# HGRN2 attention and a squared-ReLU layer on one core: chunks taken in pairs, two tokens a partition, loads in rows of 384 bytes, state products beside the score products

## The chip, the core and the metric

One core of a Trainium2 chip runs the whole kernel. The metric is the device time of one launch in microseconds. Before the change: 193.36 us, the median of three runs (192.49 to 193.87). A ratio is the mean time of one kernel's fast runs over that of the kernel before's fast runs of the same rounds on the same chip, so it isn't quite the ratio of the medians that I quote. The chips differ by about half a per cent (the fast runs of the kernel before took 192.8 us on average on one chip, 194.0 on another), so I compare experiments by their ratios.

## The reference

Four sequences of 768 tokens, 8 heads of 48. A gated linear attention, token by token, then a two-layer network over all 3072 tokens:

```python
f = 1.0 / (1.0 + np.exp(-f_logit))
for t in range(S):
    state = f[:, :, t, :, None] * state + np.einsum('bhd,bhe->bhde', k[:, :, t], v[:, :, t])
    y[:, :, t] = np.einsum('bhd,bhde->bhe', q[:, :, t], state)
# y -> x: 3072 tokens x 384
h = np.maximum(x @ w_in, 0.0)        # 384 x 2048
out = h * h @ w_out                  # 2048 x 384
```

## The kernel before

The attention goes in 24 chunks of 128 tokens. For each chunk, TensorE makes a prefix sum of the log gates (p1), ScalarE the exponentials, VectorE multiplies k and q by them; then transposes (p2), scores (p3), outputs (p4) and the state's increment (p5). Several chunks together form a unit of the two-layer network: first layer (h), relu and square on ScalarE and VectorE, second layer (o), store (d).

No engine chooses its order at run time. Each step is declared with a believed duration. A planner simulates the machine with these beliefs and writes one fixed list per engine. On the chip every engine works its list in order, and waits for data at each entry (the longest such wait of TensorE below is 3.7 us, with ready products behind it in the list):

```python
FIRST, RECEIPT = 0.4, 1.2
...
if s.data:                                   # a transfer
    us, size = s.data
    ...
    moved_to = max(moved_to, end + self.FIRST) + us     # one mover, first issued, first landed
fin = moved_to + self.RECEIPT if s.data else end + s.land
```

A load is believed to take 1.07 us and a quarter of a weight matrix 2.4 us, one behind the other. The loads are issued by SyncE, the weights by GpSimd. This is their order; `i` are quarters of the first layer's weights, `o` of the second's, numbers are chunks (f, k, q and v of each):

```python
LOADS = [0, "i0", 1, "i1", 2, "i2", 3, "i3", 4, "o0", "o1", 5, "o2", "o3"] + list(range(6, NCH))

def load(i):
    for n in ("f", "k", "q", "v"):
        def fn(n=n):
            t = io.tile([C, H, D], F32, ...)            # 1024 rows of 192 bytes
            nc.sync.dma_start(t, srcs[n][b].rearrange("h s d -> s h d")[c * C:(c + 1) * C])
        plan.add(f"{n}{i}", "SP", 0.45, fn, take=["io_" + n], rank=0, data=(1.07, 1024))
```

The state products are a step of their own, with 128 rows:

```python
def p5():
    for pr in range(NP):
        nc.tensor.matmul(ds[:, pr, :], a[:, H + 2*pr:H + 2*pr + 2, :]..., vt[:, 2*pr:2*pr + 2, :]...)
```

While TensorE has nothing ready in the first 40 us, the plan puts products of zeros ("fillers") into its list.

## Time and profile before

| profile of the kernel before | |
|---|---|
| span of the profiled run | 189.8 us |
| first first-layer product starts | 17.1 us |
| last product ends | 186.4 us |
| TensorE's products, each until the next one starts | 164.7 us |
| fillers | 13.6 us |
| gaps over 0.25 us between products | 7.0 us |

The last four lines are counted from the start times of TensorE's instructions in the trace; with the 1.0 us before the first one they add up to 186.3. The next lines are the table by stage: stretch, length, busy time (and number of instructions) of PE, PEld, DVE, ACT, POOL, then granted clock, DMA share and GB/s.

```profile
0.00:25.00 25.00, 19.48 (x238) 16.49 (x239) 15.19 (x30) 11.81 (x22) 9.96 (x26) 1.00 1.09 175
25.00:50.00 25.00, 21.95 (x330) 17.93 (x328) 17.72 (x35) 19.43 (x37) 8.14 (x14) 1.00 1.09 179
50.00:100.00 50.00, 49.64 (x568) 33.49 (x565) 43.27 (x86) 40.68 (x93) 18.22 (x33) 1.00 1.03 189
```

TensorE is full from 50 us on, and DMA moves 175 to 179 GB/s in the first two stretches. Two waits of TensorE show how it loses time in its fixed order (engine, line, what it waited for: us in total, times, longest):

```profile
PE hp L444 <- DVE hr L453: 1.9, 1, 1.9
PE pc L286 <- ACT pz L276: 1.8, 3, 1.0
```

The second is the prefix sum waiting for the gates of a later chunk. None of its three waits is over 1.0 us.

### The profile page before, as it was taken

Reading aid. Unit: us, or ns where it says so; the run is one execution under the profiler, and the core shown is the slowest. Engines: PE = TensorE matmul, PEld = TensorE weight load, DVE = VectorE, ACT = ScalarE, POOL = GpSimd, SP = SyncE. Lnnn points to the kernel's source line nnn. Section 1 sums busy time; section 2 is a strip of 40 time slices with the busy share of each in tenths; the row PEclk is TensorE's granted clock in tenths of the full one; section 3 lists DMA queues with packets and bytes.
Section 4 is the critical chain, followed back from the end, with each engine's and each line's share of the span. In section 5 each row is a group of like instructions: output and inputs, shape, how many; then the busy total and the mean of one; then the engine's idle time right before and its main releaser. Section 6 shows DMA issues by size and latency. Waiting matters only on the chain.

```text
span 189.8 us, 4807 instructions
## 1 busy us (share of the span) xinstructions
PE 177.5 (93%) x1845; PEld 120.8 (64%) x1845; DVE 127.6 (67%) x259; ACT 132.8 (70%) x281; POOL 54.8 (29%) x105
## 2 busy tenths in 40 slices
PE   6978689989899999999999999999999999999992
PEld 5867478767676666665656666666565666666551
DVE  5484688668397886999988777777667764343300
ACT  4426479786676469999998986978875787565521
POOL 5451343241224561305324311531324401100000
PEclk9999999999999999999999999999999999999999
DMA  6999899999979999999799999979999762211112
GB/s 122 188 191 206 174 187 153 196 164 191 205 137 221 232 227 201 207 197 159 140 155 194 207 137 241 218 109 215 194 216 177 176 60 64 62 45 41 41 41 83
DMA packets 118646, 30.26 MB, mean 159 GB/s; under 512 B 113408, under 2 KB 117760, under 8 KB 118624
## 3 DMA queue, kind: packets, MB, share of 16 engines
q1 hardware_dynamic: 113760, 23.27, 71.2%
q0 software_dynamic: 4864, 6.69, 16.4%
q8 instruction: 14, 0.23, 0.5%
q14 instruction: 8, 0.07, 0.1%
HBM read 25.17 MB, written 4.72 MB: 157 GB/s over the span
## 4 chain that ended last, share of the span: by engine, by line
PE 75%; ACT 11%; DMA 4%; SPq 3%; DVE 3%; issue 2%
PE op L489 31%; PE hp L444 30%; ACT hr L451 4%; DMA io_f<-in_f_logit_dram 4%; SPq L215 3%; PE at L342 3%; PE yp L365 3%; PE tr L318 2%; ACT hT L458 2%; PE pc L286 2%; PE xp L379 1%; PE ds L405 1%; ACT pz L276 1%; ACT e L275 1%; DVE hr L453 1%
## 5 line engine op out<-in xcount | busy, mean ns | idle before, releaser
L444 PE MATMUL hp<-xT,w_in 128*128 128x384 bf16 (+2 forms) x528 | 78.0, 282 | 2.5 <-DVE hr L453 1.9
L489 PE MATMUL op<-w_out,hT 128*128 128x384 bf16 x384 | 76.2, 326 | 0.3 <-ACT ob L499 0.3
L451 ACT ACTIVATE hr<-hp 128x384 bf16<-128x384 f32 (+1 forms) x100 | 50.5, 509 | 20.0 <-PE hp L444 18.0
L444 PEld LDWEIGHTS <-w_in 128*128 128x128 bf16 x528 | 42.3, 98 | 20.7 <-issue 4.0
L489 PEld LDWEIGHTS <-hT 128*128 128x128 bf16 x384 | 35.1, 98 | 21.8 <-issue 0.4
L460 DVE TENSOR_TENSOR hT<-hr 128x384 bf16<-128x384 bf16 (+1 forms) x75 | 29.7, 400 | 27.7 <-ACT hr L451 26.8
L349 DVE TENSOR_TENSOR am<-at,ut 128x512 bf16<-128x512 f32 x48 | 31.6, 685 | 3.7 <-PE at L342 3.4
L422 POOL TENSOR_TENSOR sz<-tm,en 48x192 bf16<-48x192 f32 x40 | 22.0, 549 | 29.9 <-DVE tm L413 7.2
L458 ACT ACTIVATE hT<-hr 128x384 bf16<-128x384 bf16 (+1 forms) x45 | 24.8, 554 | 1.6 <-DVE hr L453 0.3
L504 POOL DMA_DIRECT2D out_dram<-ob x18 | 10.4, 577 | 47.3 <-ACT ob L499 31.2
L280 POOL CAST vz<-io_v 128x384 bf16<-128x384 f32 x24 | 13.6, 567 | 31.2 <-DMA io_v<-in_v_dram 30.7
L306 DVE TENSOR_TENSOR az<-io_k,ep 128x384 bf16<-128x384 f32 x24 | 14.0, 584 | 8.3 <-ACT ep L296 5.1
L275 ACT ACTIVATE e<-io_f 128x384 f32<-128x384 f32 x24 | 12.5, 520 | 7.7 <-DMA io_f<-in_f_logit_dram 7.7
L499 ACT COPY ob<-op 128x384 f32<-128x384 f32 x18 | 8.6, 478 | 12.8 <-PE op L489 12.7
L296 ACT ACTIVATE ep<-pc 128x384 f32<-128x384 f32 x24 | 11.7, 486 | 5.8 <-PE pc L289 5.4
L310 DVE TENSOR_TENSOR az<-io_q,en 128x384 bf16<-128x384 f32 x24 | 14.7, 614 | 0.0
L276 ACT ACTIVATE pz<-e 128x384 bf16<-128x384 f32 x24 | 12.5, 523 | 0.8
L453 DVE TENSOR_SCALAR hr<-hp 128x384 bf16<-128x384 f32 (+1 forms) x20 | 11.6, 584 | 2.0 <-PE hp L444 1.8
L522 PE MATMUL idle<-zero 128*128 128x128 bf16 x119 | 11.9, 256 | 1.0 <-DVE zero L245 1.0
L302 ACT ACTIVATE en<-pc 128x388 f32<-128x388 f32 (+1 forms) x24 | 11.8, 491 | 0.0
L326 DVE COPY ts<-tr 128x1024 bf16<-128x1024 bf16 x14 | 9.6, 687 | 3.1 <-PE tr L318 2.7
L365 PE MATMUL yp<-vz,am 128*128 128x48 bf16 x192 | 9.5, 184 | 1.3 <-DVE am L349 0.8
(40 smaller groups left out, 149.4 us busy)
## 6 DMA issues: line engine op xcount, KB each, us to landing
io_f<-in_f_logit_dram SPq DMA_DIRECT2D x24, 192.0 KB, 4.5
io_k<-in_k_dram SPq DMA_DIRECT2D x24, 192.0 KB, 4.6
io_q<-in_q_dram SPq DMA_DIRECT2D x24, 192.0 KB, 4.5
io_v<-in_v_dram SPq DMA_DIRECT2D x24, 192.0 KB, 4.5
out_dram<-ob POOLq DMA_DIRECT2D x18, 192.0 KB, 3.5
w_in<-in_moe_w_in_dram POOLq DMA_DIRECT2D x4, 384.0 KB, 7.4
w_out<-in_moe_w_out_dram POOLq DMA_DIRECT2D x4, 384.0 KB, 6.9
out_dram<-ob SPq DMA_DIRECT2D x6, 192.0 KB, 1.9
```

The lines of the kernel that those rows point to most:

```text
L275: nc.scalar.activation(e, st["f", i].rearrange("p h d -> p (h d)"), AFT.Exp, scale=-1.0)
L276: nc.scalar.activation(pz[i % 2][:, :, :D], e.rearrange("p (h d) -> p h d", d=D), AFT.Ln, bias=1.0)
L306: nc.vector.tensor_mul(az[i % 4][:, H:, :D], st["k", i], st["ep", i])
L310: nc.vector.tensor_mul(az[i % 4][:, :H, :D], st["q", i], st["en", i][:, :HD].rearrange("p (h d) -> p h d", d=D))
L349: nc.vector.tensor_mul(t, st["at", i][x], ut4)
L365: nc.tensor.matmul(o_, w, r, start=(n == 0), stop=(n == len(ops) - 1), skip_group_check=True)
L422: nc.gpsimd.tensor_mul(nx[r, :, D * x:D * (x + 1)], st["tm", i][r, :, D * x:D * (x + 1)], st["en", i][r, HD:HD + NP].unsqueeze(2).to_broad ...
L444: nc.tensor.matmul(hp[:, x, :], w_in[:, ks, (f + x) * C:(f + x + 1) * C], xT[:, ks, lo:lo + W], start=(ks == 0), stop=(ks == KS - 1), skip ...
L451: nc.scalar.activation(hr[:, :m, :], st["hp", c0, f][:, :m, :], AFT.Relu)
L458: nc.scalar.activation(st["hT", g][:, f:f + m, lo:lo + W], hr[:, :m, :], AFT.Square)
L460: nc.vector.tensor_mul(st["hT", g][:, f:f + m, lo:lo + W], hr[:, :m, :], hr[:, :m, :])
L489: nc.tensor.matmul(st["o", i], hT[:, fs, tt * C:(tt + 1) * C], w_out[:, fs, :], start=(fs == 0), stop=(fs == FS - 1))
```

## The change

Its intent is to feed the start faster: rows of 384 bytes in place of 192, half as many loads, bigger pieces for ScalarE and VectorE, and state products that share the 64-row mode of the scores. The diff, cut to its core (cuts marked `...`):

```diff
-    LOADS = [0, "i0", 1, "i1", 2, "i2", 3, "i3", 4, "o0", "o1", 5, "o2", "o3"] + list(range(6, NCH))
+    LOADS = [0, 1, "i0", "i1", "i2", "i3", 2, "o0", "o1", "o2", "o3"] + list(range(3, NPR))   # pairs
-    XBAR = 14                                   # transposes by DMA from chunk 14
+    XBAR = 5                                    # from pair 5
-    GC = 3                                      # chunks in a unit
+    GC = 2
...
+                t = io.tile([C, H, 2, D], F32, ...)              # 1024 rows of 384 bytes
+                nc.sync.dma_start(t..., srcs[x][b][:, c*C:(c+2)*C, :].rearrange("h (p r) d -> p h (r d)", r=2))
+            plan.add(f"{x}{n}", "SP", 0.6, fn, take=["io_" + x], rank=0, data=(1.6, 1024))
...
+        def vs():                               # v's half to the other 64 partitions
+            for j in range(2):
+                nc.gpsimd.dma_start(t[b_, j]..., st["vx", n][a_]...)
+        plan.aside.add(f"vs.{n}")
+        plan.add(f"vs.{n}", "POOL", 1.2, vs, after=[f"vs0.{n}"], data=(0.33, 0), rank=-2)
...
+            if state:                           # in p3, first chunk of a pair
+                state()                         # the 16 state products of 64 rows
...
-                (nc.gpsimd if soft else nc.sync).dma_start(out[row:row + C, :], ...)
+                for r in range(2):
+                    (nc.gpsimd if soft else nc.sync).dma_start(out[row + r:row + C:2, :], st["ob", i][P2*r:P2*(r + 1)])
```

The planner itself stays the same but for `aside`: a swap's landing doesn't queue behind other transfers in its beliefs.

## The prediction

> **What bounds the kernel now.** I read the page's busy shares first, then the 40 slices, then the table by stage, then groups by shape, then the timeline.
>
> ```profile
> PE 177.5 (93%) x1845; PEld 120.8 (64%) x1845; DVE 127.6 (67%) x259; ACT 132.8 (70%) x281; POOL 54.8 (29%) x105
> ...
> PE   6978689989899999999999999999999999999992
> ...
> PEclk9999999999999999999999999999999999999999
> DMA  6999899999979999999799999979999762211112
> ...
> q1 hardware_dynamic: 113760, 23.27, 71.2%
> ```
>
> TensorE looks busy everywhere, DMA until about 150 us of 190. Both can't be the bound all the time. So I count useful TensorE work; matmuls in the first 50 us, by shape:
>
> ```profile
> L522 PE MATMUL idle<-zero 128*128 128x128 bf16 x119 | 11.9, 256 | 1.0 <-DVE zero L245 1.0
> L444 PE MATMUL hp<-xT,w_in 128*128 128x128 bf16 x150 | 10.0, 219 | 0.4 <-DVE xT L384 0.3
> L444 PE MATMUL hp<-xT,w_in 128*128 128x256 bf16 x48 | 6.4, 272 | 2.1 <-DVE hr L453 1.9 <-DVE xT L384 0.2
> L318 PE MATMUL tr<-ident,az 128*128 128x128 bf16 x48 | 4.4, 236 | 0.4 <-DVE az L310 0.4
> L489 PE MATMUL op<-w_out,hT 128*128 128x384 bf16 x19 | 4.1, 326 | 0.3 <-ACT ob L499 0.3
> ```
>
> All 119 fillers (products of zeros[...]) lie here, so part of "busy" is waiting. The means include pipeline latency; pace comes from runs of equal products in the chain and the timeline:
>
> ```profile
> 178.60 7.81 PE op L489 x48
> ```
> ```profile
> 17.11 1.47 PE L444 MATMUL hp<-xT,w_in 128*128 128x256 bf16 x12 [0.17 <-DVE xT L384]
> ...
> 21.63 0.94 POOL L280 CAST vz<-io_v 128x384 bf16<-128x384 f32 x1 [6.62 <-DMA io_v<-in_v_dram]
> ```
> ```profile
> 5.49 1.00 SPq L215 DMA_DIRECT2D io_q<-in_q_dram  x1
> 6.53 0.99 SPq L215 DMA_DIRECT2D io_v<-in_v_dram  x1
> 7.57 0.96 SPq L215 DMA_DIRECT2D io_f<-in_f_logit_dram  x1
> ```
>
> A 384-column product costs (7.81-0.326)/47 = 0.16 us; 256 columns (1.47-0.272)/11 = 0.109; 128 columns 0.056 (24 in 1.50 us at 27.54). From starts in the timeline: score block of 8 about 0.42 with the gaps around it, output block of 12 about 0.50, state product 0.045, one-column product 0.055. Useful in the first 50 us: 150 x 0.056 + 48 x 0.109 + 48 x 0.055 (transposes) + 19 x 0.16 + 6 score blocks 2.5 + 6 output blocks 2.8 + the rest 4.0 = 28.5 us. About 21 us are starved. Over the whole run: first layer 62.0 (48, 192 and 288 products of the three widths), second 384 x 0.16 = 61.4, prefix sums 8.2, transposes 6.2, scores 10.1, outputs 11.3, states 3.6, output transposes 3.0: 165.8 us. The last product ends at 178.60 + 7.81 = 186.4, so 20.6 us are not useful, the same 21. After 50 us TensorE is full; the remaining 3.4 us are the last eviction and store. So only the first 50 us can be won, and there inputs set the pace: VectorE, ScalarE and GpSimd are not full, GpSimd waited 6.62 us for a v, and the load queue issues one 192 KB load per 1.03 us, which is the rate at which they drain (191 GB/s).
>
> [...] Near 23.6 us a score block (64-row products) starts about 0.2 us after the last first-layer product's start, not 0.11[...].
>
> **The change, part by part.**
> Loads: 48 of 384 KB in place of 96 of 192 KB, same number of rows per load. [...]1.5 us each: 72 us for all, 99 before. Input and weights up to chunk 5 (4.7 + 3.1 MB) took 42 to 44 us at the 177 GB/s of the first 50 us; with about 230 GB/s some 34 us.
>
> TensorE work: first layer 576 x 0.109 = 63.1 (+1.1, three-chunk units become two-chunk ones); prefix sums 24 x 0.16 + 96 x 0.055 = 9.1 (+0.9); transposes by DMA from chunk 10 and 12 on, not 14 and 18: 80 and 36 remain, -1.8 and -1.0; state products 160 of 64 rows and 96 columns in place of 80. A score block without its gaps has (0.40-0.22)/7 = 0.026 each, with them 0.04; at 0.033 that is 5.3 (+1.7). They share the mode of the scores; the old ones needed no switch, so nothing is removed. Sum +0.9 us, on the path.
>
> VectorE: 12 subtractions x 0.55 = +6.6 us; ScalarE: one exponential less per pair, about -0.2 us x 12. Relu and square go in 96 + 96 pieces of 512, not 120 + 120: 96 x (0.594 + 0.45) = 100, before 117 over both engines. All beside TensorE. GpSimd: v copies 48 x 0.57 = 27 (13.6 before), stores 48 issues less 12 from the load queue, about 21 (10.4), swaps 24 issues x 0.5 = 12: from 55 to about 95 us. Not a bound by share, but it works in order and lies on the start.
>
> The start, step by step. The first f load took 3.1 us from issue to use, 1.03 of it transfer, so f, k, q, v of pair 0 land at 4.3, 5.8, 7.3, 8.8 us. GpSimd: two v copies to 10.0, two swap issues to 11, two more copies to 12.1, four weight issues x 0.83 to 15.4. The weights now start at 12, not 7.5, and run into pair 1's loads: v of pair 1 lands near 18[...]. The program order puts pair 1's copies and swap ahead of the first state update, so that ends at 18 + 1.1 + 1.0 + 1.1 = 21.2. Then the second chunk's output 0.5, copy 0.5, transpose 0.4, copy 0.4, waits 0.2: the first first-layer product starts near 23 us, against 17.1. By then TensorE has done 7 us (three prefix sums, four transposes, three score blocks), so 16 us are idle, against 12.7 before the first product there. After that the old kernel lost another 8; the new one gets data earlier, but in its order the transposes of pair 2 stand between first-layer blocks of pair 0 and need q of pair 2, near 32 us: I put 3 us of stalls. Idle 19, not 20.6: -1.6.
>
> End: the last store is two half transfers, +0.4. Sum: +0.9 - 1.6 + 0.4 = -0.3 us: 193.0.
>
> **The rivals.** (1) Faster input settles it: if GpSimd's order costs less (v of pair 1 lands at 15, state update done at 18), the first product starts near 20 and nothing stalls later; idle 13 to 14, time 187 to 188. For it: DMA full to 150 us, 6.62 us waits for v. Against: TensorE is full after 50 us, so later bandwidth buys nothing. (2) GpSimd becomes the chain: swap and stores ahead of state updates in its order, outputs wait for updates, TensorE stalls in order after 50 us too. For it: GpSimd sat 31.2 us waiting for ob before stores, and its load nearly doubles. Against: 95 of 190 us, and TensorE has other chunks' products. It would add 5 to 10 us: 198 to 203. (3) Four 64-row DMA transposes a pair in place of two of 128 rows: if each keeps the 1.24 us issue, the load queue has 5 + 2.4 + 3.5 = 11 us per pair of 14; loads are up to four pairs ahead, so I expect no more than 1 us.
>
> **Range and chances.** The start decides: first product at 20 to 25 us, later stalls 0 to 6 us, so idle 14 to 24 around 19, and work uncertain by 1. That gives 187.5 to 198.5. Faster by 2% needs under 189.5, idle of about 15.5 in all with the rest as summed: 0.24. Slower needs over 197.2, idle of about 23: 0.22. Within 2%: 0.54.
>
> **What would show it.** Loads: the queue's issue interval near 1.5 us and 384-byte packets at half the count. Work: first-layer groups x576, states x160 at about 0.033. Start: first product of the first layer near 23 us, with GpSimd's state update after pair 1's copies; a time near 20 points to rival 1. Full after 40 us: no stretch with TensorE much under full and no state update that the outputs wait for; if there are any, rival 2. I am wrong if the old kernel's TensorE after 50 us hides stalls that the new order removes, or if 384-byte rows drain no faster by byte than 192.

## The result and the profile after

| | before | after |
|---|---|---|
| time, median of 4 runs (us) | 192.93 (192.03 to 193.87) | 198.8 (197.9 to 199.69) |
| ratio, 95% interval | | 1.030 (1.023 to 1.038) |
| span of the profiled run | 189.8 | 197.1 |
| first first-layer product | 17.1 | 24.3 |
| products | 164.7 | 164.2 |
| fillers | 13.6 | 16.1 |
| gaps over 0.25 us | 7.0 | 11.2 |
| last product ends | 186.4 | 192.7 |

The kernel got slower, by more than my range allowed. The products take no longer; fillers and gaps make the difference. The page after, to be held against the slices in the prediction:

```profile
PE 178.5 (91%) x1951; PEld 134.3 (68%) x1951; DVE 125.8 (64%) x240; ACT 127.9 (65%) x241; POOL 92.4 (47%) x188
...
PE   8866798749999899999999999998999799999991
...
PEclk9999999957999999999999999999999999999999
```

A slice is 4.9 us. The ninth and tenth (39 to 49 us) have a clock of 0.5 and 0.7, and in the ninth TensorE is at 4 tenths. The timeline of TensorE there (start, us, engine, line, operation, operands, count, idle before and its releaser):

```profile
38.18 0.20 PE L422 MATMUL ds<-vx,az 64*128 64x96 bf16 x1
42.09 0.89 PE L333 MATMUL pc<-pz,ut 128*128 128x384 bf16 x2 [3.71 <-ACT pz L295]
42.77 0.39 PE L336 MATMUL pc<-ones,pz 128*128 128x2 bf16 x8
43.03 1.12 PE L583 MATMUL op<-w_out,hT 128*128 128x384 bf16 x3
43.94 2.77 PE L538 MATMUL hp<-xT,w_in 128*128 128x256 bf16 x12
```

TensorE stands still for 3.9 us before a prefix sum, that of pair 3. The twelve first-layer products after it take 2.77 us; in the profile before, twelve of that size took 1.47. That is the half clock: the granted clock is 1.00 from 38.0 to 40.2 us and 0.51 from 40.2 to 47.1, some 7 us at half rate (0.86 on average from 25 to 50 us). It fell 1.8 us into the gap. The length of a gap alone doesn't tell what follows: behind one of 2.4 us in e9 twelve such products took 2.77 us too, while e5, with a stall of 2.7 us, had a mean clock of 0.999. What else sets the clock is not shown. Behind the prefix sum stands ScalarE, and behind it a load:

```profile
40.64 0.84 ACT L293 ACTIVATE e<-io_f 128x768 f32<-128x768 f32 x1 [4.38 <-DMA io_f<-in_f_logit_dram]
```

The load queue tells why that f came so late (SyncE's issues; the second column is how long the queue held the issue):

```profile
8.82 1.44 SPq L224 DMA_DIRECT2D io_v<-in_v_dram  x1
10.31 1.39 SPq L224 DMA_DIRECT2D io_f<-in_f_logit_dram  x1
...
18.05 6.78 SPq L224 DMA_DIRECT2D io_f<-in_f_logit_dram  x1
24.87 5.77 SPq L224 DMA_DIRECT2D io_k<-in_k_dram  x1
30.68 5.59 SPq L224 DMA_DIRECT2D io_q<-in_q_dram  x1
```

Alone, a load of 384 KB starts every 1.47 us on average (from 7.34 to 11.75 us), 267 GB/s. The three issues from 18 us on are held for 6.05 us on average, 65 GB/s, while the eight weight transfers are in flight, from 12.7 to 40.9 us. The DMA view from 18 to 37 us shows how the queues shared (packets, MB, share of 16 engines; q0 has GpSimd's transfers, here almost all weights, q1 the loads):

```profile
q0 software_dynamic: 3158, 2.73, 86.1%
q1 hardware_dynamic: 3154, 1.19, 35.5%
```

The packets went one for one, and the load's are the smaller ones (0.38 KB on average against 0.86): the loads moved 1.19 MB in 19 us, 63 GB/s. In the chain of work that ended last (start, us, what) this is one long piece:

```profile
18.05 22.57 DMA io_f<-in_f_logit_dram
40.62 0.02 issue
40.64 0.85 ACT e L293
41.49 0.02 issue
41.51 0.53 ACT pz L295
42.05 0.04 issue
42.09 0.89 PE pc L333 x2
```

The second layer's weights were issued between 20.8 and 23.8 us, after that f, and the first quarter landed at 32.0, well before it. But the plan has one mover, first issued, first landed: it believed that f was there at 33.3 us and, behind it, put the prefix sum at 36.1 us, ahead of the first second-layer products at 36.6.

### The profile page after: what moved, and what is told of

Its sections match the earlier page's. It is cut to its first block, busy times and chain, and to the rows that moved or that the text cites.

```text
span 197.1 us, 4982 instructions
## 1 busy us (share of the span) xinstructions
PE 178.5 (91%) x1951; PEld 134.3 (68%) x1951; DVE 125.8 (64%) x240; ACT 127.9 (65%) x241; POOL 92.4 (47%) x188
## 3 DMA queue, kind: packets, MB, share of 16 engines
q0 software_dynamic: 6208, 7.87, 19.0%
## 4 chain that ended last, share of the span: by engine, by line
PE 47%; DMA 21%; SPq 10%; DVE 8%; ACT 6%; issue 5%; POOL 2%; DVEq 0%; ACTq 0%; POOLq 0%
PE op L583 22%; PE hp L538 18%; DMA io_f<-in_f_logit_dram 11%; SPq L224 9%; DMA out_dram<-ob 5%; DMA io_q<-in_q_dram 2%; DMA ts<-az 2%; PE yp L484 2%; PE pc L333 2%; DVE am L468 1%; ACT hr L545 1%; SPq L402 1%; DVE az L367 1%; PE at L458 1%; DVE hT L554 1%
## 5 line engine op out<-in xcount | busy, mean ns | idle before, releaser
L538 PE MATMUL hp<-xT,w_in 128*128 128x256 bf16 x576 | 78.5, 276 | 1.5 <-ACT xT L507 1.2
L545 ACT ACTIVATE hr<-hp 128x512 bf16<-128x512 f32 x86 | 50.6, 593 | 33.1 <-PE hp L538 30.1
L538 PEld LDWEIGHTS <-w_in 128*128 128x128 bf16 x576 | 55.0, 99 | 15.9 <-issue 2.4
L554 DVE TENSOR_TENSOR hT<-hr 128x512 bf16<-128x512 bf16 x67 | 30.6, 458 | 32.2 <-ACT hr L545 31.7
L468 DVE TENSOR_TENSOR am<-at,mask 128x512 bf16<-128x512 f32 x48 | 31.4, 679 | 3.1 <-PE at L458 3.1
L306 POOL CAST vx<-io_v 64x384 bf16<-64x384 f32 x24 | 14.8, 618 | 10.3 <-DMA io_v<-in_v_dram 9.3
L552 ACT ACTIVATE hT<-hr 128x512 bf16<-128x512 bf16 x29 | 18.2, 630 | 1.4 <-DVE hr L547 0.6
L325 POOL CAST vz<-io_v 64x384 bf16<-64x384 f32 x24 | 13.1, 547 | 1.2
L617 PE MATMUL idle<-zero 128*128 128x128 bf16 x131 | 12.4, 258 | 1.0 <-DVE zero L255 1.0
L318 POOL DMA_DIRECT2D vz<-vx x24 | 12.8, 538 | 0.0
L295 ACT ACTIVATE pz<-e 128x384 bf16<-128x384 f32 x24 | 11.2, 515 | 0.4
L617 PEld LDWEIGHTS <-zero 128*128 128x128 bf16 x131 | 10.3, 119 | 1.1 <-DVE zero L255 1.0
```

The costliest lines, as they stand in the source:

```text
L306: nc.gpsimd.tensor_copy(st["vx", n][z], vt[z, 1 - j])
L468: nc.vector.tensor_mul(t, st["at", i][x], mask.rearrange("p y s t -> p y (s t)"))
L538: nc.tensor.matmul(hp[:, x, :], w_in[:, ks, (f + x) * C:(f + x + 1) * C], xT[:, ks, lo:lo + W], start=(ks == 0), stop=(ks == KS - 1), skip ...
L545: nc.scalar.activation(hr[:, :m, :], st["hp", c0, f][:, :m, :], AFT.Relu)
L552: nc.scalar.activation(st["hT", g][:, f:f + m, lo:lo + W], hr[:, :m, :], AFT.Square)
L554: nc.vector.tensor_mul(st["hT", g][:, f:f + m, lo:lo + W], hr[:, :m, :], hr[:, :m, :])
```

## The experiments

All 18 runs, e1 to e18 in this order. They changed my theory twice. "Order" means the list of each engine. The results are right unless I say "wrong".

**First theory: the weights' burst, or the work that GpSimd got (rival).** The first run puts the second layer's weights behind pair 3:

```diff
-    LOADS = [0, 1, "i0", "i1", "i2", "i3", 2, "o0", "o1", "o2", "o3"] + list(range(3, NPR))
+    LOADS = [0, 1, "i0", "i1", "i2", "i3", 2, 3, "o0", "o1", "o2", "o3"] + list(range(4, NPR))
```

> The new kernel with the four second-layer weight transfers behind pair 2's v instead of pair 1's. Theory A (the weight burst shuts out pair 3's f load, issued at 18 and landed at 40.6 us, and TensorE then stands 3.7 us and runs two to three us at half clock): f of pair 3 in use before 32 us, no TensorE gap over 1.5 us before 50 us, mean clock back to 1.00, time 192.5 to 194.5. Theory B (what is lost is the start by pairs: first first-layer product at 24.3 us, not 17.1): that start stays and the time moves by less than 1.5, 197.5 to 200. Theory C (GpSimd's order after 50 us): the same, 197.5 to 200.

Measured: 195.97 us, ratio 1.017 (1.009 to 1.026). Pair 3's f landed at 32.1 us, its wait was gone, gaps fell to 9.2 us, but fillers rose to 17.1. About half of the loss.

The second one tells the plan alone that a weight takes longer: `data=(2.4, 0)` becomes `data=(4.0, 0)`.

> The new kernel with only the plan's belief on a weight transfer changed, 4.0 us for 2.4: the same instructions, other order. Theory A in the form that the order trusts in data too early (pair 3's prefix sum at the head of the queue while first-layer work waits behind it): the gap before that prefix sum falls under 1 us, the clock stays up, time 193.5 to 195.5, although f lands as late as before. If the missing data itself starves TensorE: the gap only moves, time 197.5 to 200.

Measured: 201.51 us, 1.047 (1.039 to 1.055). Pair 3's prefix sum, now at 50.1 us, waited for nothing (the one wait of a prefix sum for its gates that is left, 1.7 us, is pair 11's at 149 us). But the gaps after 50 us became ten, 8.1 us in all, against seven and 4.3 us in the changed kernel. The plan now believed that f there at 47.7 us, eight too late (it landed at 39.6), and everything else of the start later too. I read this as "order alone isn't the cure", which was too much: it was another false belief, on all weights at once.

The third delays the DMA transposes: `XBAR = 7`, `XBAR2 = 9` in place of 5 and 6.

> The new kernel with DMA transposes from pair 7 (scores) and 9 (outputs) on, where the kernel before has them, not 5 and 6. Theory D (the load queue stands from 59 to 74 us before pair 5's transposes, DMA runs dry and is late afterwards): the dry stretch goes, time 195 to 197.5. Otherwise TensorE gets 32 + 18 transposes more, 50 x 0.055 = 2.7 us, and the time becomes 199.5 to 202.

Measured: 200.74 us, 1.039 (1.025 to 1.052), and the same stall before pair 3's prefix sum, 2.8 us. The transposes aren't the cause.

The fourth gives the kernel before the new loads alone, 384-byte rows two chunks at a time, the rest as it was (wrong, as the tokens stand in another order):

```diff
+    t = io.tile([C, H, 2, D], F32, ...)   # one load for two chunks, each takes its half
-            plan.add(..., data=(1.07, 1024))
+            plan.add(..., data=(2.14, 1024))
```

> The kernel before with the new loads alone: 48 loads in rows of 384 bytes, chunk r of a pair taking token r of each partition, so the values are those of other tokens and the result is wrong on purpose; all else and the plan's beliefs as before. If faster input is worth something by itself (rival 1 of the prediction): first first-layer product at 15 to 17 us, time 188 to 190.5. If input is not what is missing, or coming in pairs costs what it gains: 191.5 to 194.5. Packets under 512 bytes should halve in either case.

Measured: 193.57 us, 0.998 (0.985 to 1.012). Faster rows alone are worth nothing here: the first product came later (19.7 us in place of 17.1, as a whole pair is loaded first), fillers were 14.3 us.

**Second theory: GpSimd's extra issues.** Each chunk is stored by one transfer of 128 rows (the rows of `out` in the wrong order), order unchanged:

```diff
-                for r in range(2):
-                    (...).dma_start(out[row + r:row + C:2, :], st["ob", i][P2*r:P2*(r + 1)])
+                (...).dma_start(out[row:row + C, :], st["ob", i])
```

> The new kernel with one store a chunk in place of two of 64 rows; the rows of a chunk come out in the wrong order, on purpose; the plan and every other instruction's place are unchanged. Theory C (GpSimd's in-order work after 50 us: each half store costs it 0.55 us of issue, 18 us in all, state updates and store landings behind it make TensorE's 4.3 us of gaps over 0.25 us after 50 us): those gaps fall under 2 us and the ratio to the kernel before to 1.012 to 1.022. If the gaps come from the latency of a pair instead: ratio 1.024 to 1.036 as without the edit (1.030).

Measured: 196.16 us, 1.014 (1.005 to 1.023). It looked like a hit. The trace says otherwise: the gaps (12.2 us) are no smaller than after the change, the last product ends 2.1 us earlier, and the first- and second-layer products took 2.1 us less, because the profiled run never fell to half clock (0.999 on average; its stall at 38 us was 2.7 us, not 3.9). The end is 1.0 us shorter, one store in place of two. So the 3 us were not GpSimd's issue time.

Next, no swap at all; the copies fill all 128 partitions (wrong):

```diff
-                nc.gpsimd.dma_start(t[b_, j]..., st["vx", n][a_]...)     # and the two lines around it
-        plan.add(f"vs.{n}", "POOL", 1.2, vs, after=[f"vs0.{n}"], data=(0.33, 0), rank=-2)
+        plan.add(f"vs.{n}", "POOL", 0.01, vs, after=[f"vs0.{n}"], rank=-2)
-                nc.gpsimd.tensor_copy(new_vz()[z, j], vt[z, j])
+                nc.gpsimd.tensor_copy(new_vz()[:, j], vt[:, j])
```

> The new kernel without the two transfers a pair that move v's other half across the partitions; GpSimd copies the whole 128 partitions instead, so chunks are multiplied by v of other tokens: wrong on purpose. It takes 12.8 us of issue from GpSimd and the 4.3 us landing from the way to the output products. Theory C: ratio 1.010 to 1.022. If the swap lies beside other work: 1.025 to 1.036; the first first-layer product stays at 23 to 25 us in either case, because it doesn't wait for the swap but for copies, exponentials and the second chunk's output.

Measured: 193.69 us, 1.003 (0.998 to 1.009), even better than expected. Note that the edit also changes a belief, 1.2 us to 0.01.

The state products as a step of their own again, as before the change, with 64 rows:

```diff
+            plan.add(f"p5.{n}", "PE", 0.32, p5, after=[...], take=["m0", "m1"], ...)
-            chunk(n, j, last and j == 1, rank, xbar2, None if j else p5)
+            chunk(n, j, last and j == 1, rank, xbar2, None)
```

> The new kernel with the state products as a step of their own, as in the kernel before, issued when keys and v are ready, not with the scores of the pair's first chunk (and the next pair's prefix sum kept behind them, else the plan locks up); result right. Theory E (next to the scores they wait for the transposes too, which by DMA take 3.7 us, so every state update comes late: GpSimd waits 15.4 us for the sums that feed it): that wait falls under 8 us, gaps after 50 us under 2 us, ratio 1.010 to 1.022. Rival (it saves mode changes, and the states are not what TensorE waits for): 24 more changes of mode at about 0.1 us, ratio 1.028 to 1.045.

Measured: 204.15 us, 1.058 (1.051 to 1.065), far outside of both. TensorE's stall before pair 3's prefix sum is there (3.2 us), and its seven gaps after 50 us add up to 7.1 us, against 4.3 for the changed kernel's seven. The same products in other lists cost 5 us more, 2.2 of them in the products themselves (166.4 us against 164.2; the edit also adds 24 changes between 64-row and 128-row products, for which I had estimated 0.1 us each from the profile before: near 23.6 us a score block starts 0.2 us after the first-layer product ahead of it, where these follow each other by 0.11): a first sign, no more, that the list decides.

And the edits of three runs in one kernel: late weights, one store, no swap (wrong):

```diff
+    LOADS = [0, 1, "i0", "i1", "i2", "i3", 2, 3, "o0", "o1", "o2", "o3"] + list(range(4, NPR))
+                (...).dma_start(out[row:row + C, :], st["ob", i])
+        plan.add(f"vs.{n}", "POOL", 0.01, vs, after=[f"vs0.{n}"], rank=-2)      # vs does nothing
```

> The new kernel with the second layer's weights late (the ratio went from 1.030 to 1.017 by this alone), one store a chunk and no swap; wrong on purpose. If weights and GpSimd's extra work together are the whole loss: ratio 0.995 to 1.006. If what is left after the weights is the start by pairs (about 2.5 us more filler time before the first first-layer product): 1.010 to 1.020.

Measured: 193.45 us, 1.005 (0.998 to 1.013). Inside what I expected, and yet no better than leaving out the swap alone. If GpSimd and the weights were two costs, this should have been better.

**Third theory: the order.** In the run without the swap, pair 3's f landed at 40.1 us, as late as in the changed kernel (40.6), and TensorE didn't wait for it: 12288 columns of second-layer products stood in its list before 50 us, against 4608. In its plan that f was issued 2 us later, behind the second layer's weights, and so was believed to land at 42.2 us. So I took the edit apart. First the swap gone on the chip but not in the plan (wrong), every list as in the changed kernel:

```diff
         def vs():
-                nc.gpsimd.dma_start(...)         # both
+            pass
         plan.add(f"vs.{n}", "POOL", 1.2, vs, after=[f"vs0.{n}"], data=(0.33, 0), rank=-2)   # kept
```

> The swap of v's halves over the partitions is left out (the copies fill all 128 partitions instead), but every engine's order stays that of the changed kernel; the result is wrong on purpose. The earlier run without the swap (1.003) had another order too: 12288 columns of the second layer ran before 50 us against 4608, so that the late f of pair 3 made nobody wait. Theory D, the swap itself costs (12.8 us of GpSimd's issues, 11.5 us of landing for pair 1): ratio 1.000 to 1.012, and the gap at 38 us shrinks. Theory O, the swap's place in the plan costs because of the order that follows from it: ratio 1.022 to 1.034, the 3.9 us gap before pair 3's prefix sum still there.

Measured: 200.58 us, 1.037 (1.027 to 1.047). The stall stayed:

```profile
39.27 0.20 PE L420 MATMUL ds<-vx,az 64*128 64x96 bf16 x1
41.70 0.89 PE L331 MATMUL pc<-pz,ut 128*128 128x384 bf16 x2 [2.23 <-ACT pz L295]
```

Then the swap kept on the chip but free in the plan, every list as in the run without it:

```diff
-        plan.aside.add(f"vs.{n}")
-        plan.add(f"vs.{n}", "POOL", 1.2, vs, after=[f"vs0.{n}"], data=(0.33, 0), rank=-2)
+        plan.add(f"vs.{n}", "POOL", 0.01, vs, after=[f"vs0.{n}"], rank=-2)
```

> The other half of the pair: the changed kernel with its swap, result right, but the plan believes that the swap takes 0.01 us and lands at once, so every engine has the order of the run without a swap. Theory D: the time is that of the changed kernel or worse, ratio 1.025 to 1.040, with TensorE waiting for v's half or for GpSimd. Theory O: ratio 1.000 to 1.012, near the run without a swap (1.003), no gap over 2 us before pair 3's prefix sum.

Measured: 195.43 us, 1.013 (1.004 to 1.022), just above the upper end of the theory of order. And each swap issued twice, the second time into a spare tile, order of the changed kernel:

> The changed kernel in its own order, each swap issued twice, the second time into a spare tile that nobody reads; result right. Adds 24 software DMAs on GpSimd, about 12.8 us of its time, and 2.3 MB of traffic. Theory D: GpSimd's issue time is on the path, so 2 to 6 us more than the changed kernel, ratio 1.04 to 1.06. Theory O: GpSimd still has some 80 us free, so within 1 us of the changed kernel, ratio 1.025 to 1.037.

Measured: 198.6 us, 1.027 (1.018 to 1.037). Another 12.4 us of issues on GpSimd left the total as it was, and I took the second theory for dead. But the trace shows that this null is a sum of two effects:

```profile
32.63 0.33 PE L488 MATMUL yp<-sz,ts 128*128 128x96 bf16 x4 [2.71 <-DVE tm L440]
42.97 0.50 PE L337 MATMUL pc<-pz,ut 128*128 128x384 bf16 x2
```

The list is the same, but an output now waits 2.7 us for the state, since GpSimd stood still for 5.0 us between the second layer's weights (0.7 in the changed kernel) and updated the state only after them. So TensorE came late to pair 3's prefix sum, and there it waits for nothing. More work on GpSimd does reach the path; here it took the place of the other wait. What speaks against the second theory is the run with the swap gone and the order kept: nothing was won. In that order the swap isn't what costs; its entry in the plan moved the time. In the other order (1.013 with the swap, 1.003 without, intervals that overlap) a cost of up to 1% stays open.

**Which fact of the order.** One belief alone is altered, pair 3's f lands at 40.6 us (as measured) in place of 33.3:

```diff
+    plan.told = {'f3': 40.6}
+                    fin = max(fin, end) if n not in self.told else max(end + 1.0, self.told[n])
```

> The changed kernel with one belief of its plan altered: pair 3's f lands at 40.6 us, as measured, in place of some 33 us. Order only, result right; GpSimd's order at the start is that of the changed kernel. Theory O1, this belief is the larger part of the loss: ratio 1.010 to 1.020, no gap over 1 us before pair 3's prefix sum, full clock at 40 us, first first-layer product still at 24 us. Rival, the start's order is the larger part: 1.022 to 1.030 even with that gap gone, as the lost time shows up in other gaps.

Measured: 192.87 us, 0.994 (0.987 to 1.001). More than expected: the whole loss is gone. Its clock line is full:

```profile
PE   7577787998999999989999999999999999999990
PEclk9999999999999999999999999999999999999999
```

Two runs start from the beliefs of e10: one with the late weights, one with all measured landings of the first 16 loads, the 8 weights and one swap told to the plan. Both get an order of their own.

> The order of e10 (the plan believes that the swap is free, so state update before pair 1's copies) together with the second layer's weights behind pair 3's loads (as in e1); result right. If the two gains add: e10 1.013 less e1's 0.013 = ratio 0.997 to 1.004. If both only remove the same wait for pair 3's f: 1.010 to 1.017, like e10 alone.

> As e10, and the plan is told the landing times measured in the changed kernel for the first 16 loads and the 8 weights; order only, result right. If right beliefs make a good order: ratio 1.003 to 1.013, gaps before 50 us under 4 us in all. If beliefs are not what decides and orders scatter by chance: 1.015 or more.

Measured: 196.71 us, 1.015 (1.006 to 1.025), and 196.83 us, 1.016 (1.009 to 1.024). Neither is better than e10. The late weights add nothing once the wait is gone; fillers rose to 21.2 us. And more right beliefs don't make a better order by themselves: in the second, gaps of 2.2 and 1.4 us came up at 115 and 118 us.

The control: the kernel before, its plan given the false belief of the second run (a weight takes 4.0 us).

> Control: the kernel before, its plan told that a weight takes 4.0 us in place of 2.4 (the edit of e2, which cost the changed kernel 1.047 against 1.030); order only, result right. If sensitivity to false beliefs is a property of the static order: ratio 1.015 to 1.04. If it is the change's own (few large pieces, few chunks in flight): 0.995 to 1.010.

Measured: 199.32 us, 1.028 (1.021 to 1.036). One false belief costs the kernel before as much as the change did. The sensitivity isn't the change's own.

**The wait alone.** The run with one belief altered had another order to its very end, so a lucky order elsewhere was still possible. Here the list of the changed kernel is kept, and only the seven steps of pair 3's gates stand 6 us later in it:

```diff
+    plan.moved = {x + ".3" for x in ("a1", "p1", "a2p1", "a2n1", "sub", "a2p0", "a2n0")}
+                    if n in self.moved:
+                        at[-1] += 6.0
-        return res
+        return [res[x] for x in sorted(range(len(res)), key=lambda x: (at[x], x))]
```

> The changed kernel in its own order, except that the seven steps of pair 3's gates (softplus, prefix sum, subtraction, four exponentials) stand 6 us later in the order, behind products that are ready; nothing else moves, result right. If the in-order wait for pair 3's f is the whole cause (3.9 us of gap and about 2 us of half clock): ratio 0.995 to 1.008. If e12's gain came from the later order: 1.015 to 1.030, other gaps taking its place.

Measured: 194.13 us, 1.003 (0.997 to 1.009). TensorE at the same place, with second-layer products where the stall was:

```profile
38.90 0.20 PE L427 MATMUL ds<-vx,az 64*128 64x96 bf16 x1
39.03 0.66 PE L588 MATMUL op<-w_out,hT 128*128 128x384 bf16 x3
39.53 1.47 PE L543 MATMUL hp<-xT,w_in 128*128 128x256 bf16 x12
...
44.75 0.49 PE L338 MATMUL pc<-pz,ut 128*128 128x384 bf16 x2
```

The prefix sum stands at 44.75 us and waits for nothing, and twelve first-layer products take 1.47 us again. Between 25 and 50 us the two kernels differ like this, first the changed kernel, then this one:

```profile
25.00:50.00 25.00, 20.54 (x244) 15.77 (x243) 15.85 (x31) 15.23 (x29) 7.14 (x14) 0.86 1.21 234
```
```profile
25.00:50.00 25.00, 24.10 (x291) 19.32 (x289) 19.45 (x38) 18.53 (x36) 9.90 (x19) 1.00 1.16 228
```

Forty-seven more TensorE instructions are in the records of that stretch at nearly the same DMA rate. TensorE's list, read from the two traces, differs in the place of that prefix sum and in nothing else. The mean clock of the two profiled runs doesn't tell them apart (0.983 and 0.982): this one fell to half clock too, but from 8.4 to 15.3 us, before the first first-layer product.

Then another late belief, 44.0 us in place of 40.6, which makes another whole order:

> As e12, but the plan believes 44.0 us in place of 40.6; another whole order, result right. If a late enough belief is all that is needed: ratio 0.990 to 1.008. If 0.994 was one lucky order among scattered ones: 1.010 to 1.030.

Measured: 195.06 us, 1.008 (1.001 to 1.015). So 0.994 was somewhat lucky, and 1.003 and 1.008 are its neighbours; all three are without the stall, and the three lie around the kernel before.

The last try was for a right kernel that beats both: e12's order and one store for each chunk, its target rearranged so that the rows come out right.

```diff
+                (...).dma_start(out[row:row + C, :].rearrange("(p r) d -> r p d", r=2), st["ob", i])
```

> e12's order, and each chunk stored by one transfer of 128 rows with a rearranged target, so the result is right. If GpSimd's extra store issues and the second half at the end still cost: 1 to 3 us less than e12, ratio 0.980 to 0.990. If only the end counts: 1.0 us less than e12, about 0.989. If neither: 0.994.

Measured: 231.63 us, 1.188 (1.175 to 1.202); the result is right. The software queue's packets rose from 6208 to 11104; in the trace 5292 of them are of 12 bytes, a size that the run with two stores doesn't have. The stores land later, after 8.5 us in place of 3.8; why is not shown, as the trace's records as I read them don't tell which engine carried what. The transfers beside it slow down too, the DMA transposes from 3.7 us to 7.8. The DMA lists (target and source, issuer, count, KB each, median us to landing), first of e12, then of this run:

```profile
out_dram<-ob POOLq DMA_DIRECT2D x36, 96.0 KB, 3.8
...
ts<-az SPq DMA_TRANSPOSE x28, 3.7
```
```profile
out_dram<-ob POOLq DMA_DIRECT2D x18, 192.0 KB, 8.5
...
ts<-az SPq DMA_TRANSPOSE x28, 7.8
```

So whether GpSimd's extra store issues cost anything once the wait is gone stays open; this form of the store hides it.

## Why the prediction was wrong

The sum in the prediction was +0.9 (work) - 1.6 (idle) + 0.4 (end). By the traces:

| us | predicted | after the change | pair 3's gates moved (e16) |
|---|---|---|---|
| products, against before | +0.9 | -0.5 | -1.7 |
| fillers and gaps, against before | -1.6 | +6.8 | +2.7 |
| of these before the first first-layer product | 16 in all | 18.0 in all | 17.5 in all |
| of these after it | 3 in all | 10.3 in all | 6.8 in all |
| end, last product to end of span, against before | +0.4 | +1.0 | +1.0 |

**The loads: right.** 1.47 us for 384 KB were measured, 1.5 predicted; per byte 1.47 us against 2 x 1.04 is 0.71. Packets fell from 118646 to 77335. The first 50 us ran at 223 and 234 GB/s on average, and I had put 230. Both the 1.5 and the 230 were my estimates, which no trace had shown by then. Beside the weights the longer rows won little: 63 GB/s from 18 to 37 us, 267 alone, where the rows of 192 bytes had got 55 GB/s (0.44 MB from 10 to 18 us in the kernel before, 2330 packets against 1117 of the other queue), 191 alone.

**The start: nearly right.** The first first-layer product came at 24.3 us, 23 predicted. Pair 1's v landed at 15.1 us, earlier than the 18 I had estimated, but the product still waited 1.2 us for the transposed copy on ScalarE.

**The work: right in size.** The state products took 5.2 us in all, 5.3 predicted. Scores took 6.9 us against 8.1 before, which I had left out. The 96 two-column products cost 0.029 us each, where I had put 0.055; but the 80 one-column products of before cost 0.027, so the error is in both and hardly counts in the difference. One product is wrong in the sum: 576 x 0.109 is 62.8, not 63.1, so the work should have come to +0.6; the 0.3 us decide nothing.

**The step that failed** is "I put 3 us of stalls", and the sentence ahead of it, "the new one gets data earlier". What the runs showed in its place is 10.3 us, and 1.9 us more in first- and second-layer products at half clock (128.8 us for both layers, 126.9 with the gates moved). I looked for the stall at the transposes of pair 2 and its q. It was pair 3's f. I had the total of the bandwidth right, but not who gets it: while weights were in flight, the load queue got 63 to 65 GB/s, so a load issued 2.7 us before the second layer's weights landed after three of their four quarters, 8.6 us after the first. The plan believes in first come, first served, and put the prefix sum ahead of work that was ready. Moving those seven steps and nothing else took the ratio from 1.030 to 1.003. In the profiled spans it is 197.1 to 191.8 us: 4.0 us of gaps, and 1.2 us of products. That is the cause of 5.3 of the 7.2 us, and it is shown. The chain behind it, a false belief that orders the list, is shown by the altered belief (e12) and by the run without the swap that kept list and stall (e9).

The stall is not all that the 3 us missed: with the gates moved, 6.8 us of idle are still there after the first first-layer product. "After 50 us TensorE is full" did not carry over to the new lists either: the gaps over 0.25 us after 50 us are 0.7 us before, 4.3 after the change and 4.3 with the gates moved. The longest, 1.1 us, waits for a DMA transpose at 153 us; no run here takes these gaps away, so their cause is not shown.

Of the rest, +2.5 us are fillers (the first product comes 7 us later) and +0.2 gaps, against 1.7 us less of products, and the second half store adds 1.0 us at the end. This leaves the pairing a draw, which is what e16, e12 and e17 measured (1.003, 0.994, 1.008). My 193.0 would have been near these, but not by its steps: more idle, less work.

**The rivals.** The second one, GpSimd becomes the chain, named 198 to 203 us and seemed to be confirmed. It is not: with the swap gone and the order kept, the time stayed at 1.037, and with the swap there and seven steps moved it fell to 1.003. (The doubled swap is no proof, as its trace shows.) A right number was no proof of its mechanism. The first, faster input settles it, fell with e4: the loads alone gave 0.998. The third, the transposes' issue, was small: later transposes made it no faster.

**What stays open.** Why orders without a wait at pair 3's prefix sum still scatter from 0.994 to 1.047 (e2; 1.027 for the doubled swap) I can't say from one fact; each has its own gaps. To lose the stall was no guarantee: only e16 takes it away and leaves the rest of the list alone. The clock's share in single runs isn't settled either: of the changed kernel's twin with two swaps, the run with 0.991 took 199.74 us and one with 0.977 took 198.02.

## What to carry to other kernels

In a kernel with a fixed order, a change of the code is also a change of the order; before you explain a loss by the new instructions, run the new instructions in the old order and the old ones in the new order, and give a false belief to the old kernel as a control. When a transfer is asked for by two queues, don't predict from the total bandwidth when a certain tile lands, but look up in the trace what its queue gets while the other is busy (here 63 to 65 GB/s, and 267 alone). Here seven steps moved by 6 us in a list were worth nearly all that the change had lost. And read the trace of a run that changed nothing, too: the doubled swap had lost one wait and gained another.
